# Streaming attention over a key and value cache: K tiles loaded one tile ahead of V tiles, and P V moved to the end of the next group's scores

## The chip, the cores and the metric

The kernel runs on one core of one Trainium2 chip. The metric is the device time of the kernel in microseconds (us), as the median of several executions. "Span" below is the time inside one profiled execution; it is 1.8 to 1.9 us shorter than the time of the same execution in every run here. "Granted clock" is the share of its full clock that the tensor engine was granted.

## The reference, cut to what matters

```python
# B = 8 sequences, one query each; H = 32 heads, Sk = 4096 keys, Dh = 128, D = 576; bf16
q = (x @ wq).reshape(B, 1, H, Dh).transpose(0, 2, 1, 3)
scores = einsum("bhqd,bhkd->bhqk", q, k_cache) * Dh ** -0.5
o = einsum("bhqk,bhkd->bhqd", softmax(scores), v_cache)
a = o.transpose(0, 2, 1, 3).reshape(B, 1, H * Dh) @ wo
# b: a small MLP with a layernorm, D -> 4608 -> D
return g * a + (1 - g) * b          # g = sigmoid((x * gate_w).sum(-1))
```

The K and V caches are 268 MB each and are read once. The weights are 20 MB in all. Everything else is small.

## The kernel before

The work is cut into 64 groups, each of one sequence and four heads. A group has one K tile and one V tile of 4 MB each, `[128 partitions, 128, 128]` in bf16. There are two K buffers and two V buffers (`g % 2`). All large loads go out in program order from one queue, that of the sync engine (SP).

Scores are computed in four chunks. For each, the vector engine (DVE) multiplies K by the query (`mult`), eight matmuls of the tensor engine (PE) with the identity sum up parts of the products, and DVE reduces the rest (`reduce`). `softmax` finds the maximum on DVE and takes exponentials on the scalar engine (ACT). Then come, for the same group: `rowsum` (DVE) and `total` (PE) for the denominator; `pv`, 32 matmuls of P with V (PE); `evict` (ACT), which copies their result out of PSUM, the memory that matmuls write to; `gather` (PE) and `norm` (DVE), which put it together and divide.

```python
def load_k(g):                       # waits until the multiplies of group g-2 are done
    s = g % 2
    k_land[g] = op("sync", lambda e: e.dma_start(KB[s][:, :, :], src), [k_done.get(g - 2)], dma=(sK[s], ...))
def load_v(g):                       # waits until P V of group g-2 is done
    t = op("sync", lambda e: e.dma_start(VB[s][:, :, :], src), [v_done.get(g - 2)], dma=(sV[s], ...))
# load_v_pieces(g): the last V tile, in four pieces of 64, 32, 16 and 16 of its 128 rows per partition

def scores(g, between):
    mult(g, 0); between(0)
    mult(g, 1); between(1)
    for c in range(NCK):             # NCK = 4
        reduce(g, c)
        if c + 2 < NCK:
            mult(g, c + 2); between(c + 2)

K_AHEAD = NG - 2                     # 62; NG = 64
for g in range(NG):
    if g == K_AHEAD - 1:   load_k(g); load_k(g + 1); load_v(g)
    elif g == K_AHEAD:     load_k(g + 1); load_v(g)
    elif g > K_AHEAD:      load_v_pieces(g)
    elif g >= 2:           load_k(g); load_v(g)

    def between(c, g=g):
        if c == 0 and 1 <= g < K_AHEAD:  pv(g - 1, 0, 1); evict(g - 1)
        if c == 1 and g >= 1:            rowsum(g - 1); total(g - 1)
        if c == 2 and 1 <= g < K_AHEAD:  gather(g - 1)       # + MLP parts (cut)
        if c == 3 and 1 <= g < K_AHEAD:  norm(g - 1)         # + MLP parts (cut)
    scores(g, between)
    softmax(g)
    if g >= K_AHEAD:
        pv(g - 1, 0, 1); evict(g - 1); gather(g - 1); norm(g - 1)
    # ... a_proj when eight groups are done (cut)
rowsum(NG - 1); total(NG - 1); pv(NG - 1, 0, 1); evict(NG - 1); gather(NG - 1); norm(NG - 1)
# last a_proj, two vector operations, one store (cut)
```

Tiles are named by group below: K63 and V63 are the last ones.

## Time and profile before

| | before |
|---|---|
| time, median of 3 | 1322.35 us |
| span of the profiled execution | 1321.4 us |
| bytes read | 557 MB |
| one 4 MB tile on the DMA engines | 9.71 us |
| last V piece lands | 1304.05 us |
| end of the span after it | 17.3 us |

The page's row of DMA busy tenths and of GB/s, in 40 equal slices of the span, of the kernel before:

```profile
DMA  9999999999999999999999999999999999999993
GB/s 398 428 429 428 429 434 430 434 429 427 434 431 430 435 428 422 422 435 430 430 431 430 430 433 430 431 431 429 429 436 430 431 430 430 430 432 435 405 430 159
```

DMA is busy nearly everywhere. Only the last slice is not full.

The windows view of the kernel before: stretches in us from the span's start, busy time of each engine with the number of instructions, granted PE clock, DMA share, GB/s:

```profile
60.00:500.00 440.00, 288.10 (x1851) 136.32 (x1851) 286.75 (x348) 71.82 (x134) 0.00 (x0) 0.81 1.00 431
620.00:1200.00 580.00, 367.80 (x2258) 162.56 (x2257) 400.02 (x477) 94.50 (x179) 0.00 (x0) 0.82 1.00 431
1246.00:1252.00 6.00, 4.43 (x25) 2.43 (x23) 4.79 (x8) 0.28 (x1) 0.00 (x0) 1.00 0.78 309
1310.88:1321.40 10.52, 6.28 (x50) 3.06 (x50) 2.05 (x6) 0.60 (x1) 0.00 (x0) 0.70 0.01 2
```

In the middle DMA runs at 431 GB/s with a share of 1.00, while PE and DVE are busy for two thirds of the time. There is one dip near 1250 us, and almost nothing is moved in the last 10 us.

The waits view of the kernel before, "who waited for whom: us in total, times, longest":

```profile
DVE p L343 <- DMA KB<-in_A_k_cache_dram: 190.8, 58, 16.0
```

The page's list of DMA issues of the kernel before: count, KB each, median us from issue to landing:

```profile
KB<-in_A_k_cache_dram SPq DMA_DIRECT2D x64, 4096.0 KB, 26.1
VB<-in_A_v_cache_dram SPq DMA_DIRECT2D x63, 4096.0 KB, 21.1
```

DVE, the busiest engine, waits for the next K in nearly every group: the loads set the pace. A tile itself needs 9.71 us, so a V is issued with some 11 us of other loads ahead of it (21.1 - 9.7).

The end of the timeline of the kernel before: start and duration in us, engine, line, output <- inputs, count, and in brackets the idle time of the engine before it and what ended it:

```profile
1270.88 4.45 DVE L343 TENSOR_TENSOR p<-KB,q_bc 128x4096 bf16<-128x4096 bf16 x2
...
1285.63 2.33 ACT L385 ACTIVATE P<-s_sb,mD 32x128 bf16<-32x128 f32 x4 [1.65 <-DVE mD L382]
1287.99 0.60 ACT L416 ACTIVATE O_sb<-psb 128x512 f32<-128x512 f32 x1
1288.64 1.87 PE L421 MATMUL psb<-sel,O_sb 128*128 128x4 f32 x8 [3.13 <-ACT O_sb L416]
1290.55 0.18 DVE L427 RECIPROCAL rz<-psb 128x4 f32<-128x4 f32 x1 [4.95 <-PE psb L421]
...
1290.84 4.49 DVE L343 TENSOR_TENSOR p<-KB,q_bc 128x4096 bf16<-128x4096 bf16 x2
...
1306.49 2.33 ACT L385 ACTIVATE P<-s_sb,mD 32x128 bf16<-32x128 f32 x4 [17.90 <-DVE mD L382]
1308.85 0.60 ACT L416 ACTIVATE O_sb<-psb 128x512 f32<-128x512 f32 x1
...
1310.88 0.68 DVE L391 TENSOR_REDUCE rs<-P 128x4 f32<-128x512 bf16 x1
1312.13 3.32 PE L403 MATMUL psb<-VB,P 128*16 128x512 bf16 x32
```

L343 is `mult`: at 1270.88 that of group 62, at 1290.84 that of group 63. K63 had landed at 1284.5, so group 63 starts 6 us late. The chain that holds it stands above it: exponentials of group 62 on ACT (L385), then the eviction of P V of 61 on the same engine (L416), its gather (L421), and its norm, for which DVE sits idle for 4.95 us. After group 63's exponentials the same small steps of group 62 come again before `rowsum` of 63 (L391).

### The profile page before, as it was taken

Reading aid. Unit: us, or ns where it says so; the run is one execution under the profiler, and the core shown is the slowest. Engines: PE = TensorE matmul, PEld = TensorE weight load, DVE = VectorE, ACT = ScalarE, POOL = GpSimd, SP = SyncE. Lnnn points to the kernel's source line nnn. Section 1 sums busy time; section 2 is a strip of 40 time slices with the busy share of each in tenths; the row PEclk is TensorE's granted clock in tenths of the full one; section 3 lists DMA queues with packets and bytes.
Section 4 is the critical chain, followed back from the end, with each engine's and each line's share of the span. In section 5 each row is a group of like instructions: output and inputs, shape, how many; then the busy total and the mean of one; then the engine's idle time right before and its main releaser. Section 6 shows DMA issues by size and latency. Waiting matters only on the chain.

```text
span 1321.4 us, 12174 instructions
## 1 busy us (share of the span) xinstructions
PE 834.4 (63%) x5204; PEld 376.9 (29%) x5204; DVE 873.5 (66%) x1058; ACT 211.2 (16%) x394; POOL 2.3 (0%) x11
## 2 busy tenths in 40 slices
PE   3538768676366686357656756665755765675666
PEld 1224334333132332123223322322322322232223
DVE  4547666667476677466666766766766767676674
ACT  1201111112111111011111111111111111111111
POOL 0000000000000000000000000000000000000000
PEclk8778788778787887688788778878778877888887
DMA  9999999999999999999999999999999999999993
GB/s 398 428 429 428 429 434 430 434 429 427 434 431 430 435 428 422 422 435 430 430 431 430 430 433 430 431 431 429 429 436 430 431 430 430 430 432 435 405 430 159
DMA packets 24726, 557.76 MB, mean 422 GB/s; under 512 B 2368, under 2 KB 6496, under 8 KB 7008
## 3 DMA queue, kind: packets, MB, share of 16 engines
q1 hardware_dynamic: 24496, 556.95, 98.4%
q8 instruction: 41, 0.67, 0.2%
q14 instruction: 13, 0.11, 0.0%
q10 hardware_dynamic: 176, 0.03, 0.0%
HBM read 556.96 MB, written 0.01 MB: 422 GB/s over the span
## 4 chain that ended last, share of the span: by engine, by line
DMA 63%; PE 22%; DVE 14%; ACT 0%; issue 0%; SPq 0%
DMA KB<-in_A_k_cache_dram 63%; PE psb L353 15%; DVE p L343 11%; PE psb L403 6%; DVE s_sb L358 2%; PE psb L421 0%; ACT P L385 0%; PE psb L441 0%; ACT O_sb L416 0%; DVE mA L376 0%; PE psb L487 0%; DVE rz L427 0%; DVE mB L378 0%; SPq L183 0%; DVE gm L379 0%
## 5 line engine op out<-in xcount | busy, mean ns | idle before, releaser
L353 PE MATMUL psb<-p,ident 128*128 128x512 bf16 x2048 | 595.8, 445 | 461.6 <-DVE p L343 461.6
L343 DVE TENSOR_TENSOR p<-KB,q_bc 128x4096 bf16<-128x4096 bf16 x256 | 579.4, 2284 | 190.8 <-DMA KB<-in_A_k_cache_dram 190.8
L353 PEld LDWEIGHTS psb<-p,ident 128*128 128x128 bf16 x2048 | 208.1, 111 | 765.2 <-DVE p L343 490.6
L358 DVE TENSOR_REDUCE s_sb<-psb 128x32 f32<-128x512 f32 x256 | 176.2, 689 | 223.6 <-PE psb L353 223.6
L385 ACT ACTIVATE P<-s_sb,mD 32x128 bf16<-32x128 f32 x256 | 146.9, 574 | 122.4 <-DVE mD L382 120.0
L403 PE MATMUL psb<-VB,P 128*16 128x512 bf16 x2048 | 150.1, 445 | 0.0
L416 ACT ACTIVATE O_sb<-psb 128x512 f32<-128x512 f32 x64 | 38.2, 597 | 536.9 <-PE psb L403 536.9
L337 ACT ACTIVATE q_bc<-psb 128x128 bf16<-128x128 f32 x64 | 17.7, 277 | 424.8 <-PE psb L335 424.8
L403 PEld LDWEIGHTS psb<-VB,P 128*16 128x16 bf16 x2048 | 49.7, 100 | 116.2 <-issue 88.0
L421 PEld LDWEIGHTS psb<-sel,O_sb 128*128 128x128 f32 x512 | 67.8, 194 | 17.5 <-ACT O_sb L416 8.7
L421 PE MATMUL psb<-sel,O_sb 128*128 128x4 f32 x512 | 62.0, 244 | 7.0 <-ACT O_sb L416 7.0
L391 DVE TENSOR_REDUCE rs<-P 128x4 f32<-128x512 bf16 x64 | 43.4, 679 | 0.0
L410 PEld LDWEIGHTS psb<-rs,ones 128*128 128x128 f32 x128 | 24.4, 192 | 10.2 <-DVE rs L391 1.2
L427 DVE RECIPROCAL rz<-psb 128x4 f32<-128x4 f32 x64 | 11.3, 176 | 14.8 <-PE psb L421 14.8
L441 PE MATMUL psb<-yT_sb,RB 128*128 128x8 bf16 (+1 forms) x216 | 20.0, 228 | 0.0
L376 DVE TENSOR_REDUCE mA<-s_sb 128x1 f32<-128x128 f32 x64 | 18.3, 286 | 2.2
L441 PEld LDWEIGHTS psb<-yT_sb,RB 128*128 128x128 bf16 (+1 forms) x216 | 19.2, 169 | 1.0
L410 PE MATMUL psb<-rs,ones 128*128 128x4 f32 x128 | 18.3, 213 | 1.1 <-DVE rs L391 1.1
L378 DVE STREAM_TRANSPOSE mB<-mA 128x32 f32<-128x32 f32 x64 | 13.6, 212 | 2.2
L382 DVE STREAM_TRANSPOSE mD<-mC 128x32 f32<-128x32 f32 x64 | 13.6, 212 | 2.2
L335 PE MATMUL psb<-Q,Sel 128*128 128x128 bf16 x64 | 14.3, 224 | 0.0
L379 DVE TENSOR_REDUCE gm<-mB 128x1 f32<-128x32 f32 x64 | 11.9, 186 | 2.2
(56 smaller groups left out, 89.6 us busy)
## 6 DMA issues: line engine op xcount, KB each, us to landing
KB<-in_A_k_cache_dram SPq DMA_DIRECT2D x64, 4096.0 KB, 26.1
VB<-in_A_v_cache_dram SPq DMA_DIRECT2D x63, 4096.0 KB, 21.1
RB<-in_B_w_dram SPq DMA_DIRECT2D x1, 5184.0 KB, 28.0
RB<-in_B_w_dram SPq DMA_DIRECT2D x1, 4608.0 KB, 47.0
RB<-in_A_wo_dram SPq DMA_DIRECT2D x1, 4608.0 KB, 28.3
RB<-in_A_wq_dram SPq DMA_DIRECT2D x1, 4096.0 KB, 12.5
VB<-in_A_v_cache_dram SPq DMA_DIRECT2D x1, 2048.0 KB, 13.6
VB<-in_A_v_cache_dram SPq DMA_DIRECT2D x1, 1024.0 KB, 15.7
```

Of the source, the lines that this page charges most:

```text
L337: a_qb[g] = op("scalar", lambda e: e.activation(out=q_bc[:, g % 2, :], in_=qb_ps[:, 0:DH], func=ACT.Copy), [t, v_mult.get((g - 2, NCK - 1))])
L343: v_mult[g, c] = op("vector", lambda e: e.tensor_tensor(out=p1[:, par, :, :], in0=KB[s][:, c * CT:(c + 1) * CT, :], in1=qb, op=ALU.mult), ...
L353: p_sum[g, c] = op("tensor", lambda e, r=r, n=n: e.matmul(tr_ps[par][:, :], lhsT=ident[:, :], rhs=r, start=(n == 0), stop=(n == NCH - 1)), w)
L358: v_red[g, c] = op("vector", lambda e: e.tensor_reduce(out=s_sb[:, s, c * CT:(c + 1) * CT], in_=tr_ps[par][:, :].rearrange("p (t c) -> p t ...
L376: t = op("vector", lambda e: e.tensor_reduce(out=mA[:, 0:1], in_=s_sb[:, s, :], axis=AX.X, op=ALU.max), [v_red[g, NCK - 1], c_mA])
L385: a_exp[g] = op("scalar", lambda e, h=h, q=q: e.activation(out=P[q, s, :, h], in_=s_sb[q, s, :], func=ACT.Exp, bias=mD[q, s, 0:1], scale=1.0),
L391: v_rs[g] = op("vector", lambda e: e.tensor_reduce(out=rs[:, s, :], in_=P[:, s, :, :].rearrange("p t h -> p h t"), axis=AX.X, op=ALU.add), ...
L403: p_pv[g] = op("tensor", lambda e, o=o, tq=tq: e.matmul(o, lhsT=P[:, s, tq * TQ:(tq + 1) * TQ, :].rearrange("p t h -> p (t h)"), rhs=VB[s] ...
L410: p_z[g] = op("tensor", lambda e: e.matmul(oz_ps[:, HB:2 * HB], lhsT=ones[:, :], rhs=rs[:, g % 2, :], start=True, stop=True), [v_rs[g], v_ ...
L416: a_ev[g] = op("scalar", lambda e: e.activation(out=O_sb[:].rearrange("p t d -> p (t d)"), in_=o_ps[s][:, :], func=ACT.Copy), [p_pv[g], p_ ...
L421: p_oz[g] = op("tensor", lambda e, tt=tt: e.matmul(oz_ps[:, 0:HB], lhsT=O_sb[:, tt, :], rhs=sel16[:, tt, :], start=(tt == 0), stop=(tt == ...
L441: st["p_up"] = op("tensor", lambda e, w=w, o=o, kt=kt: e.matmul(o, lhsT=w, rhs=yT_sb[:, kt, :], start=(kt == 0), stop=(kt >= NKF)), [*ld_w ...
```

## The change

Its intent: load K(g+1) ahead of V(g) in every group, not only in the last ones, and do P V of group g-1 behind the last score chunk of group g, with its gather and norm in group g+1. Then the special case at the end disappears.

```diff
@@ first loads
     load_k(1)
-    load_v(1)
@@ main loop
-        if g == K_AHEAD - 1:   load_k(g); load_k(g + 1); load_v(g)
-        elif g == K_AHEAD:     load_k(g + 1); load_v(g)
-        elif g > K_AHEAD:      load_v_pieces(g)
-        elif g >= 2:           load_k(g); load_v(g)
+        if g >= 1:
+            if g + 1 < NG:     load_k(g + 1); load_v(g)
+            else:              load_v_pieces(g)
@@ between(c)
-            if c == 0 and 1 <= g < K_AHEAD:  pv(g - 1, 0, 1); evict(g - 1)
+            if c == 0 and g >= 2:            gather(g - 2)
             if c == 1 and g >= 1:
                 rowsum(g - 1)
+                if g >= 2: norm(g - 2)
                 total(g - 1)
-            c == 2, 1 <= g < K_AHEAD:  gather(g - 1)
-            c == 3, 1 <= g < K_AHEAD:  norm(g - 1)
+            c == 3, g >= 1:            pv(g - 1, 0, 1); evict(g - 1)
@@ after softmax(g)
-        if g >= K_AHEAD: pv(g - 1, 0, 1); evict(g - 1); gather(g - 1); norm(g - 1)
@@ after the loop
+    gather(NG - 2); norm(NG - 2)
     rowsum(NG - 1); total(NG - 1); pv(NG - 1, 0, 1); ...
```

(Several statements are joined on one line here. Also cut: the MLP parts start one group later, and the projection of eight finished groups moves into a score chunk.) The number of instructions and of bytes does not change.

More of the change, by code (lines that the diff above doesn't have):

```diff
@@ L489, in a_proj @@
                     start=(h == 0), stop=(h == H - 1)), [v_norm[hg * B + B - 1], st["ld_wo"], st["v_bx"]])
-    UP0, UPN = 2, 12
-    DN0, DNN = 18, 6
+    UP0, UPN = 3, 12
+    DN0, DNN = 19, 6
     AP0 = 28
-    K_AHEAD = NG - 2
     q_of(0)
-    done_a = 0
+    done_a = [0]
     for g in range(NG):
-        if g == K_AHEAD - 1:
-            load_k(g)
-            load_k(g + 1)
-            load_v(g)
-        elif g == K_AHEAD:
-            load_k(g + 1)
-            load_v(g)
-        elif g > K_AHEAD:
-            load_v_pieces(g)
-        elif g >= 2:
-            load_k(g)
-            load_v(g)
+        if g >= 1:
+            if g + 1 < NG:
+                load_k(g + 1)
+                load_v(g)
+            else:
+                load_v_pieces(g)
         def between(c, g=g):
-            if c == 0 and g >= 1:
-                if g < K_AHEAD:
-                    pv(g - 1, 0, 1)
-                    evict(g - 1)
+            if c == 0 and g >= 2:
+                gather(g - 2)
             if c == 1 and g >= 1:
                 rowsum(g - 1)
+                if g >= 2:
+                    norm(g - 2)
                 total(g - 1)
             if c == 2:
-                if 1 <= g < K_AHEAD:
-                    gather(g - 1)
                 if UP0 <= g < UP0 + UPN:
@@ L526, in between @@
                     down_proj((g - DN0) * NJ // DNN, (g - DN0 + 1) * NJ // DNN)
+                if g >= AP0 and done_a[0] * B + B + 1 <= g:
+                    a_proj(done_a[0])
+                    done_a[0] += 1
             if c == 3:
-                if 1 <= g < K_AHEAD:
-                    norm(g - 1)
+                if g >= 1:
+                    pv(g - 1, 0, 1)
+                    evict(g - 1)
                 if g == UP0 + UPN:
@@ L542, in bass_gated_mix__mha_block_cached__mixer_channel_mlp__decode_kernel @@
         softmax(g)
-        if g >= K_AHEAD:
-            pv(g - 1, 0, 1)
-            evict(g - 1)
-            gather(g - 1)
-            norm(g - 1)
-        if g >= AP0 and (done_a + 1) * B <= g:
-            a_proj(done_a)
-            done_a += 1
+    gather(NG - 2)
+    norm(NG - 2)
     rowsum(NG - 1)
@@ L556, in bass_gated_mix__mha_block_cached__mixer_channel_mlp__decode_kernel @@
     norm(NG - 1)
-    while done_a < NHG:
-        a_proj(done_a)
-        done_a += 1
+    while done_a[0] < NHG:
+        a_proj(done_a[0])
+        done_a[0] += 1
     last = []
```

## The prediction

> **What bounds it now.** DMA. The page shows 557 MB moved and DMA busy 9 tenths or more in 39 of 40 slices; the windows view gives share 1.00 at 431 GB/s from 60 to 500 and from 620 to 1200 us, close to the 435 GB/s ceiling in the specifications of the Trainium skill's page "DMA: Bandwidth & Descriptors". A 4 MB tile takes 9.71 us (spacing of landings), a group 19.4 us. The timeline of a middle group runs 16.2 us from K's landing (610.03) to the end of softmax; DVE then waits for the next K: 190.8 us in 58 waits (waits view). Compute has slack in every group, so moving PV, gather and norm cannot speed up the stream.
>
> Only the end is not DMA-bound. The last V piece lands at 1304.05 (semaphore increments in the trace), but the span ends at 1321.4. These 17 us are compute, and late: K63 lands at 1284.5, but its first multiply starts at 1290.84, because DVE waits 4.95 us for gather and norm of group 61, which stand behind group 62's exponentials and an eviction on ACT. After group 63's exponentials (1308.82) come eviction, gather and norm of group 62 before rowsum of 63 (1310.88); rowsum to the end costs 10.5 us.
>
> **What the change does.** Instructions and bytes stay.
> - Middle: K(g+1) is issued when group g-1's multiplies are done, so the queue is deeper. No gain: before, about 11 us of work is already ahead of each V issue, 16 us ahead of each K. Gather of g-2 now stands between the first two score sums, and norm ahead of the first reduce: about +1 us per group (0.95 on PE, 0.4 on DVE), so 17 us, up to 18 with up-projection. Below 19.4: hidden.
> - A DMA dip vanishes: 289 and 328 GB/s at 1246 to 1252 us, when K62 is issued late (1248.8; it waits for group 60's multiplies). I give it little value: K61's 16 increments come from 1246.81 to 1254.43, so only early engines ran dry. The skill's page (section on why a DMA increments its semaphore by 16) says engines finish independently and only the full 16 means landed; the trace agrees, with spreads of 0.2 us at the start and 7.6 us late. The slowest engine sets the end.
> - End: load order from K62 on is the same, so K63 still lands near 1284.5, V63 near 1304. K61 lands one tile earlier, so group 62 is done by 1282 and group 63 starts at 1284.5 (-6.3 us). Its softmax takes 1.5 us longer (gather and norm of 61 inside), exponentials end near 1304.7 (evict 62 ahead, 0.6), and rowsum follows without eviction, gather and norm of 62 (-2 us). End: 1304.7 + 10.5 = 1315.3 by the profile, 6 us less.
>
> All of that gain is on the critical path; DMA's end is not moved.
>
> **Predicted:** 1316.2 us, 8 in 10 between 1312 and 1320. Faster by over 2%: 0.01; within 2%: 0.98; slower: 0.01.
>
> **What would show it.** 431 GB/s unchanged in the middle; K landings 19.4 us apart; K63's multiply starts on its DMA near 1284; last V lands 1303 to 1305; 11 to 12 us from there to the end (17 before); K landing to softmax about 17 us.
>
> **What would make it wrong.** Another spread of the engines moves K63 and V63 by 1 or 2 us. If a group exceeded 19.4 us, DVE would bound: slower. If the starved engines at 1246 us did set the end, 2 to 4 us more are won.

## The result, and the profile after

The changed kernel took 1317.92 us (median of 4), the kernel before 1322.6 us beside it: ratio 0.996 (0.994 to 0.998). In a second set of rounds it took 1317.58 us with ratio 0.995 (0.993 to 0.996). The prediction was 1316.2 us, 1312 to 1320.

By the 2% that counts as a difference here, the two kernels are the same; the difference is small but clear of the noise.

The page's row of GB/s of the changed kernel:

```profile
GB/s 398 428 429 430 431 430 429 429 430 433 432 429 431 433 428 430 420 427 430 430 430 430 432 430 432 433 431 430 431 430 431 430 430 429 431 432 431 432 433 190
```

The windows view of the changed kernel, the same stretches (the last one from `rowsum` of group 63 to the end, as before):

```profile
60.00:500.00 440.00, 308.59 (x1868) 156.15 (x1868) 292.86 (x349) 70.28 (x135) 0.00 (x0) 0.79 1.00 431
620.00:1200.00 580.00, 399.48 (x2262) 186.10 (x2263) 401.28 (x474) 90.19 (x177) 0.00 (x0) 0.81 1.00 431
1246.00:1252.00 6.00, 5.14 (x21) 2.62 (x22) 4.31 (x6) 0.00 (x0) 0.00 (x0) 0.72 0.99 426
1304.64:1316.90 12.26, 8.06 (x50) 4.12 (x50) 2.05 (x5) 0.60 (x1) 0.00 (x0) 0.51 0.01 2
```

The middle is as before, 431 GB/s at share 1.00. The dip at 1250 us is gone, yet the last V piece lands at 1303.65 us, against 1304.05 before.

The waits view of the changed kernel:

```profile
DVE p L342 <- DMA KB<-in_A_k_cache_dram: 174.8, 62, 16.3
```

The page's list of DMA issues of the changed kernel:

```profile
KB<-in_A_k_cache_dram SPq DMA_DIRECT2D x64, 4096.0 KB, 26.0
VB<-in_A_v_cache_dram SPq DMA_DIRECT2D x63, 4096.0 KB, 31.6
```

A V now stands in the queue 10 us longer before it lands (31.6 us against 21.1): the queue is deeper, and the loads end only 0.4 us sooner. DVE waits a little less, as each group takes it a little longer.

The end of the timeline of the changed kernel:

```profile
1263.93 4.49 DVE L342 TENSOR_TENSOR p<-KB,q_bc 128x4096 bf16<-128x4096 bf16 x2 [2.77 <-DMA KB<-in_A_k_cache_dram]
...
1284.12 4.49 DVE L342 TENSOR_TENSOR p<-KB,q_bc 128x4096 bf16<-128x4096 bf16 x2 [2.70 <-DMA KB<-in_A_k_cache_dram]
...
1291.60 0.18 DVE L426 RECIPROCAL rz<-psb 128x4 f32<-128x4 f32 x1 [2.39 <-PE psb L420]
...
1301.66 0.60 ACT L415 ACTIVATE O_sb<-psb 128x512 f32<-128x512 f32 x1 [17.21 <-PE psb L402]
1302.28 2.33 ACT L384 ACTIVATE P<-s_sb,mD 32x128 bf16<-32x128 f32 x4
...
1304.64 0.69 DVE L390 TENSOR_REDUCE rs<-P 128x4 f32<-128x512 bf16 x1 [0.85 <-ACT P L384]
...
1305.91 3.59 PE L402 MATMUL psb<-VB,P 128*16 128x512 bf16 x32
```

Group 63's multiply (1284.12) now starts on its own load. The idle time before it ends with DMA, not with a small operation of an older group. Norm of 61 sits inside group 63 (DVE idle 2.39 us), and nothing stands between the exponentials and `rowsum`.

A second profile of the same kernel (`after_again` below) differs in one place, its windows view from `rowsum` of 63 to the end:

```profile
1304.70:1315.20 10.50, 6.28 (x50) 3.13 (x50) 2.05 (x5) 0.60 (x1) 0.00 (x0) 0.68 0.01 2
```

The same 50 matmuls took 6.28 us here and 8.06 us above; the granted PE clock was 0.68 against 0.51. No run here shows what decides which of the two an execution gets.

So the difference of the spans, taking the execution with the same clock at the end (1321.4 to 1315.2 us), is a sum of three terms:

| stretch | before | after_again | difference |
|---|---|---|---|
| start of group 63's multiply | 1290.84 | 1284.06 | -6.8 |
| from there to the end of its exponentials | 18.0 | 20.6 | +2.6 |
| from there to `rowsum` of 63 | 2.1 | 0.0 | -2.0 |
| `rowsum` of 63 to the end | 10.5 | 10.5 | 0.0 |
| sum | | | -6.2 |

### The profile page after: what moved, and what is told of

It reads as the page before. It is cut to its first block, busy times and chain, and to the rows that moved or that the text cites. A ratio compares the mean times of both kernels' runs of the same rounds, so it can differ in the third digit from the quotient of the medians.

```text
span 1316.9 us, 12176 instructions
## 1 busy us (share of the span) xinstructions
PE 897.5 (68%) x5204; PEld 428.9 (33%) x5204; DVE 871.6 (66%) x1058; ACT 204.5 (16%) x394; POOL 2.3 (0%) x11
## 4 chain that ended last, share of the span: by engine, by line
DMA 64%; DVE 18%; PE 17%; ACT 1%; issue 0%; SPq 0%
DMA KB<-in_A_k_cache_dram 64%; DVE p L342 14%; PE psb L352 13%; PE psb L420 3%; DVE s_sb L357 3%; PE psb L402 1%; ACT P L384 0%; DVE rz L426 0%; DVE OT_sb L427 0%; ACT O_sb L415 0%; PE psb L486 0%; SPq L183 0%; ACT L455 0%; DVE rs L390 0%; PE psb L409 0%
## 5 line engine op out<-in xcount | busy, mean ns | idle before, releaser
L352 PE MATMUL psb<-p,ident 128*128 128x512 bf16 x2048 | 651.1, 476 | 398.5 <-DVE p L342 398.5
L352 PEld LDWEIGHTS psb<-p,ident 128*128 128x128 bf16 x2048 | 226.4, 121 | 713.0 <-DVE p L342 430.6
L402 PE MATMUL psb<-VB,P 128*16 128x512 bf16 x2048 | 123.5, 383 | 0.0
L420 PEld LDWEIGHTS psb<-sel,O_sb 128*128 128x128 f32 x512 | 106.1, 287 | 24.5 <-issue 16.7
L420 PE MATMUL psb<-sel,O_sb 128*128 128x4 f32 x512 | 92.1, 303 | 1.4 <-ACT O_sb L415 1.4
L402 PEld LDWEIGHTS psb<-VB,P 128*16 128x16 bf16 x2048 | 45.9, 90 | 71.8 <-issue 28.4
L409 PEld LDWEIGHTS psb<-rs,ones 128*128 128x128 f32 x128 | 31.3, 245 | 18.0 <-issue 9.5
L409 PE MATMUL psb<-rs,ones 128*128 128x4 f32 x128 | 21.1, 235 | 2.0 <-DVE rs L390 2.0
L440 PEld LDWEIGHTS psb<-yT_sb,RB 128*128 128x128 bf16 (+1 forms) x216 | 19.4, 165 | 3.3
L334 PEld LDWEIGHTS psb<-Q,Sel 128*128 128x128 bf16 x64 | 6.1, 95 | 27.3 <-issue 26.7
## 6 DMA issues: line engine op xcount, KB each, us to landing
VB<-in_A_v_cache_dram SPq DMA_DIRECT2D x63, 4096.0 KB, 31.6
```

Of the source, the lines that this page charges most:

```text
L334: t = op("tensor", lambda e: e.matmul(qb_ps[:, 0:DH], lhsT=Sel[:, b, :], rhs=Q4[:, hg * DH:(hg + 1) * DH], start=True, stop=True), [a_Q[hg ...
L352: p_sum[g, c] = op("tensor", lambda e, r=r, n=n: e.matmul(tr_ps[par][:, :], lhsT=ident[:, :], rhs=r, start=(n == 0), stop=(n == NCH - 1)), w)
L402: p_pv[g] = op("tensor", lambda e, o=o, tq=tq: e.matmul(o, lhsT=P[:, s, tq * TQ:(tq + 1) * TQ, :].rearrange("p t h -> p (t h)"), rhs=VB[s] ...
L409: p_z[g] = op("tensor", lambda e: e.matmul(oz_ps[:, HB:2 * HB], lhsT=ones[:, :], rhs=rs[:, g % 2, :], start=True, stop=True), [v_rs[g], v_ ...
L420: p_oz[g] = op("tensor", lambda e, tt=tt: e.matmul(oz_ps[:, 0:HB], lhsT=O_sb[:, tt, :], rhs=sel16[:, tt, :], start=(tt == 0), stop=(tt == ...
L440: st["p_up"] = op("tensor", lambda e, w=w, o=o, kt=kt: e.matmul(o, lhsT=w, rhs=yT_sb[:, kt, :], start=(kt == 0), stop=(kt >= NKF)), [*ld_w ...
```

## The experiments

One number is not printed by the views but stands in the trace. Each load raises its semaphore 16 times, once for each of the 16 DMA engines that carry it. The times of these increments tell when the earliest and the slowest engine finished a tile. The Trainium skill's page "DMA: Bandwidth & Descriptors" (section "Why a DMA increments its semaphore by 16 and not by 1") says that the engines finish independently, and that only the full 16 means landed. The trace agrees: in the kernel before, the first and last increment of a tile are 0.2 us apart at K0 and 7.6 us apart at K61. "Spread" below is that distance, and "lead" is how long before the slowest engine finished the load ahead of it a load was issued.

The theory: only the end of the kernel is faster; the loads end when the slowest engine ends, and that engine always had work queued. The rivals: the deeper queue, the vanished dip or the rearranged middle is what gained.

### 1. after_again: the changed kernel as control

> The changed kernel again, as a control beside the others on the same chip. Both theories: 0.995 to 0.997 of the kernel before. In the profile: K63's multiply starts at its landing near 1284, last V piece near 1304, rowsum of group 63 near 1304.7; rowsum to the end of the span between 10.5 and 12.3 us, longer when the last matmuls fall into a stretch of half clock.

Measured: 1317.58 us, ratio 0.995 (0.993 to 0.996). `rowsum` at 1304.70, last V piece 1303.54, 10.5 us from `rowsum` to the end. As expected.

### 2. mid_only: the new middle with the old end

```diff
+    T = NG - 5
-        if g >= 1: ...                        # new order throughout
+        if 1 <= g < T:  load_k(g + 1); load_v(g)
+        elif g == T:    load_v(g)
+        elif g == T+1:  load_k(g); load_v(g)
+        ...                                   # 61, 62, 63 as in the kernel before
```

P V, gather and norm follow: the new places up to `T`, the old ones after it.

> New order of loads and new place of P V up to group 58, then the old end (K61 and K62 together, P V of 61 and 62 after the softmax). Theory 'the end alone': no gain, 0.999 to 1.001 of the kernel before, K63's multiply late again (near 1290.8, behind norm of group 61), rowsum near 1310.9. Rival 'the deeper queue or the rearranged middle feeds the DMA better': most of the gain, 0.996 to 0.997, last V piece earlier than 1303.

Measured: 1324.56 us, ratio 1.000 (0.998 to 1.001). Timeline of mid_only:

```profile
1288.22 0.60 ACT L415 ACTIVATE O_sb<-psb 128x512 f32<-128x512 f32 x1
1290.18 0.18 DVE L427 TENSOR_TENSOR OT_sb<-psb,rz 128x4 bf16<-128x4 f32 x1
1290.26 4.49 DVE L342 TENSOR_TENSOR p<-KB,q_bc 128x4096 bf16<-128x4096 bf16 x2
...
1310.30 0.68 DVE L390 TENSOR_REDUCE rs<-P 128x4 f32<-128x512 bf16 x1
```

Group 63 starts behind norm of 61 again, and the last V piece lands at 1304.02, not before 1303 as the rival had it. Some 59 of 64 groups run the new way, and nothing is gained. The rival falls.

### 3. tail_only: the old middle with the new end

The mirror image: `T = NG - 6`, the old loads and places up to it, the new ones after it. At the change-over K58 and K59 are loaded together, so K59 is issued late, as K62 was in the kernel before.

> Old order and old place of P V up to group 57, new ones from group 58 on. K59 is issued late, as K62 was before, so the early engines run dry once here too. Theory 'the end alone': all of the gain, 0.995 to 0.997 of the kernel before, last V piece still near 1304 in spite of the dip, K63's multiply at its landing near 1284. Rival 'the middle, or the vanished dip': no gain, 0.999 to 1.001.

Measured: 1317.58 us, ratio 0.995 (0.993 to 0.996), the same as the whole change. Timeline of tail_only:

```profile
1284.00 4.49 DVE L343 TENSOR_TENSOR p<-KB,q_bc 128x4096 bf16<-128x4096 bf16 x2 [3.57 <-DMA KB<-in_A_k_cache_dram]
...
1303.91 0.69 DVE L391 TENSOR_REDUCE rs<-P 128x4 f32<-128x512 bf16 x1 [0.86 <-ACT P L385]
```

The dip was there: the early engines ran dry and the spread fell from 7.6 us (K58) to 3.9 us (V58). The last V piece landed at 1303.54 all the same, where after_again, without a dip, has 1303.54. The slowest engine needed 9.71 us for K59 as for any tile. So all of the gain is in the last groups, and this dip cost nothing. The run also keeps the MLP parts and the projection where they were, so their move gained nothing either. One small thing stays open: the two kernels with a late K62, before and mid_only, have their last V piece at 1304.05 and 1304.02, while after_again and tail_only have it at 1303.54. K62 took the slowest engine 10.7 and 10.5 us there; no run tells whether its late issue or one of the steps named in the last section did that. It is 0.5 us at most.

### 4. order_only: the new order of loads alone

The kernel before with the first hunk and the load hunk of the change; P V stays where it was.

> The kernel before with the new order of loads alone; P V stays behind the first score chunk (after the softmax in the last two groups). P V of g-1 now waits for V of g-1, which lands 9.7 us after K of g, and holds the second score sum. Theory 'the end alone': K landing to end of softmax grows from 16 to about 20.5 us, 1 us over the 19.4 us of a group's loads, but it starts anew at each landing, so nothing adds up; K61 lands a tile earlier, group 63 starts about 1285.5, and eviction, gather and norm of 62 still stand before rowsum (about 1306): 0.995 to 0.998 of the kernel before. Rival 'the new place of P V keeps the middle from being bound by compute': 1 us per group adds up, 1.02 or more.

Measured: 1321.44 us, ratio 0.9975 (0.996 to 0.999). No loss adds up in the middle (431 GB/s, last V piece 1303.48). Timeline of order_only:

```profile
1287.18 4.49 DVE L342 TENSOR_TENSOR p<-KB,q_bc 128x4096 bf16<-128x4096 bf16 x2
...
1307.30 0.67 DVE L390 TENSOR_REDUCE rs<-P 128x4 f32<-128x512 bf16 x1
```

Group 63 starts 3.7 us earlier than before, 3.1 us later than after the change. About half of the gain belongs to the order of loads. The other half, from `rowsum` at 1307.30 to 1304.70, is put down to the new place of P V by difference only: no run has it alone in the last groups. The kernel runs a little later than I expected (1285.5 and 1306), because group 61, which still waits for V60 inside its second chunk, ends at 1267.1, after K62 has landed.

### 5. pv_only: the new place of P V alone

The changed kernel with the load hunks undone, so K(g) and V(g) alternate as before.

> The changed kernel with the old order of loads: only P V, gather and norm move. V of g+1 waits for P V of g-1, now about 17 us after K of g landed, with 2.4 us of loads left on the slowest engine and none on the earliest. Theory 'only the slowest engine counts': the early engines run dry in every group, so the spread of landings collapses to 2 or 3 us, and the slowest loses only where a group is late (half clock, up-projection): last V piece 1304 to 1310, K63's multiply near 1288 at best; 0.997 to 1.005 of the kernel before. Rival 'idle engines cost time': each group loses the 4 to 6 us that its early engines idle for, 1.05 or more. Either way the new place of P V needs the new order of loads.

Measured: 1378.71 us, ratio 1.040 (1.038 to 1.043): outside the ranges of both theories, nearer to the rival's. The profiled execution was the slowest of six (1385.88 us). The page's list of DMA issues of pv_only:

```profile
VB<-in_A_v_cache_dram SPq DMA_DIRECT2D x63, 4096.0 KB, 14.5
```

The windows view of pv_only:

```profile
60.00:500.00 440.00, 287.96 (x1757) 145.24 (x1753) 271.57 (x327) 67.32 (x129) 0.00 (x0) 0.78 0.98 411
```

The last V piece lands at 1366.96 us, 63 us later than after the change: the loads themselves became slower. The DMA share still reads 0.98. A V now takes 14.5 us from issue to landing, of which 9.7 us are its own: less than 5 us of loads is queued ahead of it, against 11 before. The early engines did run dry, and the spread fell to 2 or 3 us, as expected. But the slowest engine lost about 1 us per V too (10.75 us from landing to landing in place of 9.75). Its lead was 3.5 us in the median and 1.3 us at worst. I had taken it that any lead above zero is enough for the slowest engine. That is wrong here; the next run asks whether the lead is the cause.

### 6. pv_third: the same with P V one chunk earlier

```diff
+            c == 2, g >= 1: pv(g - 1, 0, 1); evict(g - 1)
-            c == 3, g >= 1: pv(g - 1, 0, 1); evict(g - 1)
```

> pv_only with P V one score chunk earlier (behind the third sum instead of the fourth), so that V is issued about 3 us earlier, with 5 us or more of loads left on the slowest engine instead of 2.4 to 3. Theory 'pv_only lost because V was issued less than about 3.5 us before the slowest engine ran dry': the loss is gone, though the early engines still run dry: 0.996 to 1.002 of the kernel before, spread of landings below 5 us, last V piece 1303 to 1306, 32 KB packets back near 1.22 us on average. Rival 'idle early engines, or gather and norm in the wrong place, cost the time': still 1.02 or more.

Measured: 1330.13 us, ratio 1.004 (1.003 to 1.006). The loss of the loads is nearly gone: the last V piece lands at 1307.68, 4 us late instead of 63 (1303 to 1306 was expected). The spread stays below 5 us (2.2 in the median) and the 32 KB packets take 1.22 us on average, both as expected; in pv_only they took 1.25. The median lead of V is 5.2 us. On the earliest engine it is 2.8 us, and that engine still loses a little at each V (9.9 us from first increment to first increment, where 9.7 is free of loss); the slowest one does not. The ratio just misses the expected range, because K61 lands at 1259.1 and the last three groups then run one after the other at the pace of compute: group 63 starts only at 1295.37.

The loads of runs 4 to 9 and of both kernels together, 960 K and V tiles (the first and last few left out), grouped by lead (worked out from issue times and increments; "spacing" is the mean time from the slowest engine's end of the load ahead to its end of this one):

```
lead (us)    tiles   spacing (us)
below 2.5       14   11.8
2.5 to 3         4   11.3
3 to 3.5        15   10.8
3.5 to 4         8   10.6
4 to 5          39    9.9
5 to 8          41    9.8
8 to 15        207    9.8
above 15       632    9.8
```

In these kernels, a load that was issued less than about 4 us before the slowest engine ran dry mostly cost time. Beyond that, a deeper queue gave nothing. It is no sharp limit: 8 of the 39 tiles between 4 and 5 us took 10.1 us or more, and 5 of the 41 below 4 us lost nothing. It also rests on few kernels: of these 41 tiles, 38 are V tiles of pv_only and 3 of pv_third. The kernel before has 10 us or more at every whole V, 8.7 us at the first piece of the last one and 5.7 us at its worst K (K62), which is why the change's deeper queue gained nothing.

Part of the 4 us can be seen. In the kernel before, some seven engines had run dry when K62 was issued at 1248.78; the packet records show their first 32 KB packets starting 1.0 to 1.6 us later, and several of them taking 1.6 to 2.3 us where 1.21 us is usual. That makes up to some 2.7 us; the rest of the 4 us stays open.

### 7. k63_early: K63 ahead of V61 and V62

Only group 63's own chain stands between K63 and the end, so its tile can come sooner and two V tiles later.

```diff
-        if g >= 1: load_k(g + 1); load_v(g)   (or the last pieces)
+        if 1 <= g < NG - 3:  load_k(g + 1); load_v(g)
+        elif g == NG - 3:    load_k(g + 1)
+        elif g == NG - 2:    load_k(g + 1); load_v(g - 1); load_v(g)
@@ group 63
+            c == 0: pv(61); evict(61); load_v_pieces(63)
+            c == 1: gather(61)      c == 3: norm(61); total(62); pv(62); evict(62)
```

> Meant to beat both: the changed kernel with K63 loaded ahead of V61 and V62, and P V of 61 moved into group 63. Early engines run dry near 1256 and 1286. Theory 'the slowest engine sets the end of the loads': K63 lands near 1274, group 63's exponentials end near 1300, last V piece still near 1304, and only the last piece's P V, eviction, gather, norm, projection and store follow: 7 to 9 us, so 1311 to 1314 us in all, 0.991 to 0.994. Rival 'idle engines cost time': the last V piece lands 2 to 5 us later than 1304, and the time is 1315 or more.

Measured: 1314.00 us, ratio 0.9915 (0.990 to 0.993). Timeline of k63_early:

```profile
1281.56 4.45 DVE L342 TENSOR_TENSOR p<-KB,q_bc 128x4096 bf16<-128x4096 bf16 x2
...
1301.89 0.69 DVE L390 TENSOR_REDUCE rs<-P 128x4 f32<-128x512 bf16 x1 [0.86 <-ACT P L384]
...
1310.47 0.31 SPq L183 DMA_DIRECT2D out_dram<-out_sb  x1
```

K63 landed at 1274.2, and group 63 starts right behind group 62. The early engines ran dry twice: the spread went from 7.4 us (K62) to 4.4 us (K63) and to 1.5 us (V63). The last V piece landed at 1303.54 as in after_again. Idle early engines cost nothing again. The lead was 5.6 us at K63 and only 3.4 us at the first piece of V63, which lost nothing all the same: it landed 4.89 us after V62, as in after (4.86).

### 8. k63_early2: P V of 61 one chunk later

```diff
-            c == 0: pv(61); evict(61); load_v_pieces(63)
-            c == 1: gather(61)
+            c == 1: pv(61); evict(61); load_v_pieces(63)
+            c == 2: gather(61)
@@ after the loop
     rowsum(63)
-    total(63)
     pv(63); evict(63)
+    total(63)
```

> K63 ahead of V61 and V62 as in k63_early, with P V of 61 behind the second score sum instead of the first, gather of 61 behind the third, and the total of 63 behind its P V instead of ahead of it. The last V pieces are issued about 1291.5, later than before, which by the theory costs nothing while the slowest engine is still at V62 (till 1293.7). Group 63's softmax ends 1 to 2 us earlier and P V of 63 starts about 1300 to 1301 instead of 1302.9, ending within 1 us of the last V piece (1303.5 to 1304.5): 1 to 2.5 us less than k63_early, 0.989 to 0.991. Rival: the late issue moves the last V piece past 1305, and nothing is won.

Measured: 1314.23 us, ratio 0.992 (0.991 to 0.994): nothing won, as the rival said. Timeline of k63_early2:

```profile
1301.17 1.04 PE L402 MATMUL psb<-VB,P 128*16 128x512 bf16 x16 [1.40 <-ACT P L384]
...
1306.14 0.60 PE L402 MATMUL psb<-VB,P 128*16 128x512 bf16 x4 [0.64 <-DMA VB<-in_A_v_cache_dram]
```

P V of 63 starts at 1301.2 instead of 1302.9, but its last part waits for the last V piece, which lands at 1306.09. The pieces were issued at 1291.75 with a lead of 2.9 us, against 1290.23 and 3.4 us in k63_early.

### 9. v63_in_kb: the last V goes into a free K buffer

```diff
-            dst = VB[s][...]        waits for P V of 61
+            dst = KB[1 - s][...]    waits for the multiplies of 62
```

On top of k63_early2; P V of 63 reads that buffer.

> k63_early2, but the last V goes into the K buffer that group 62 has left, so its load waits for group 62's multiplies (about 1277) instead of P V of 61 (1291.7). Theory: the lead of V63's issue over the slowest engine is 15 us again, its last piece lands at 1303.5 to 1304.5 instead of 1306.1, P V of 63 follows the pieces, and 5.7 to 8 us later (by the granted clock) all is done: 1311 to 1313.5 us, 0.990 to 0.992, 0.5 to 3 us below k63_early2. Rival: the last V piece still lands past 1305.5, so the late issue was not the cause.

Measured: 1313.06 us, ratio 0.991 (0.990 to 0.992). Timeline of v63_in_kb:

```profile
1277.96 1.76 SPq L183 DMA_DIRECT2D KB<-in_A_v_cache_dram  x4
...
1301.55 1.69 PE L403 MATMUL psb<-KB,P 128*16 128x512 bf16 x28 [1.40 <-ACT P L384]
1303.80 0.39 PE L403 MATMUL psb<-KB,P 128*16 128x512 bf16 x4 [0.57 <-DMA KB<-in_A_v_cache_dram]
...
1309.09 0.31 SPq L183 DMA_DIRECT2D out_dram<-out_sb  x1
```

The pieces are issued 14 us earlier and the last one lands at 1303.76: the late issue was the cause in run 8. The landings show it; the times of runs 8 and 9 alone would not, as their intervals overlap. It is the fastest kernel, though not clear of k63_early, which was timed in another set of rounds (0.9897 to 0.9924 against 0.9901 to 0.9928). Its end is set by the load: four matmuls and the final steps stand behind the last piece.

## Why the prediction was right or wrong

- "Compute has slack in every group, so moving PV, gather and norm cannot speed up the stream": right. The middle stays at 431 GB/s, and mid_only gained nothing (1.000).
- "K landing to softmax about 17 us": right in the mean. In the middle of the changed kernel one group takes 18.1 us (600.33 to 618.39) and the next 16.8 us (619.75 to 636.52). Over groups 20 to 57 the mean is 17.3 us (longest 18.2), where the kernel before has 17.0, so the cost was 0.4 us per group and not the "about +1 us" of the prediction. The groups with up-projection (3 to 14) took up to 18.5 us. The prediction had no term for the group behind them: group 15, with the vector steps of the MLP, took 22.6 us, over the 19.4, and group 16 started 3.2 us late; the next groups started on their loads again.
- "A DMA dip vanishes. I give it little value": right. tail_only has such a dip and the whole gain.
- "The slowest engine sets the end": right for the changed kernel and in runs 3 and 7. It has a limit that the prediction did not state: it held while the load was issued about 4 us or more ahead (3.4 us in run 7). In pv_only it was not, and all engines lost. The prediction's "if the starved engines did set the end, 2 to 4 us more" did not come true.
- "K63 still lands near 1284.5, V63 near 1304", "group 63 starts at 1284.5": measured 1284.10, 1303.65 and 1284.12.
- "Exponentials end near 1304.7, rowsum follows": measured 1304.6 and 1304.64. Within it, the softmax of group 63 grew by 2.0 us (17.6 against 15.6 to the end of DVE's part), not 1.5. That 0.5 us was made up by K63, which landed 0.4 us earlier than assumed, so to meet 1304.7 this closely was in part luck.
- "Rowsum to the end costs 10.5 us": this term of the sum was mis-sized for the profiled execution. It took 12.3 us there and 10.5 us in the second profile, with the same instructions and a granted clock of 0.51 and 0.68. In the nine profiles where the same steps follow `rowsum` it took 10.3 to 10.5 us in four and 12.3 us in five, never between, so the predicted 1315.3 for the span was met by one profile (1315.2) and missed by 1.6 us by the other.
- The step from the span to the time was mis-sized too: I set the span of 1321.4 against the median of 1322.35, a distance of 0.9 us, while the execution that was profiled took 1323.21. With the true distance of 1.8 us the forecast would have been 1317.1, against medians of 1317.9 and 1317.6.

What is left open: the kernel before varied from 1322.2 to 1327.9 us over the sets of rounds, the changed one only from 1316.7 to 1318.8. No run here tells why, and the gain in per cent (0.4 to 0.55) depends on it.

## What to carry to other kernels

When the loads fill the whole span, look for the gain where they have ended: read what the last tile's work waits for, and move older groups' small steps out of its way. Order the last loads so that the tile with the longest work behind it lands first, and the one with the shortest work last. A deeper queue gains nothing once each load is issued some 4 us before the slowest DMA engine runs dry, but a reordering of compute that delays the release of a buffer can cut that lead and cost far more (here 4%) than the end can give; so change the order of loads and the place of the releasing work together.

## What the Trainium skill lacked or had wrong

- "DMA: Bandwidth & Descriptors", section "Where 436 GB/s comes from", says that for transfers between HBM and SBUF the HBM side (about 358 GB/s) binds. Here one core read 431 GB/s from HBM for over 1,000 us, within 1% of the page's other ceiling of 435 GB/s. The page itself marks the numbers of its table of measured loads as those of a single core with the other core of its pair idle, and gives half of the HBM for two cores that stream; the sentence on what binds leaves this out.
- The same page advises to issue a DMA early, but says nothing on how early a load must be in the queue so that it costs nothing behind another one. The runs show about 4 us before the slowest engine runs dry, with scatter: mean spacing 9.8 to 9.9 us above that, 10.6 to 11.8 us below, and no loss in one load at 3.4 us.
- The same page does not tell how far the 16 engines drift apart over a long stream of loads. Here the spread of one tile's 16 increments grew from 0.2 us to 7.6 us. Some steps come right after a 16 KB packet of the instruction queue in the packet records (at 279.9 us, spread 2.0 to 3.2; at 795.3 us, 4.7 to 6.0 in the kernel before); that these packets cause the drift was not tested.
- "TensorE: Matmul & The Clock Gate", Part 1, describes the clock gate that follows the recent activity of PE by a free-running window. The runs agree with it (in after_again the granted clock goes from half to full and back at 1308.55 and 1311.96 us, 3.41 us apart) and add a number for a short end: the same 50 matmuls behind the loads took 6.3 or 8.1 us, at a granted clock of 0.68 or 0.51, so the same kernel ended 1.8 us earlier or later.
